# A fused attention and expert kernel: the listed order of every engine worked out anew, instructions unchanged

## The chip, the cores and the metric

One core of a Trainium2 chip runs the kernel. The metric is the device time of one execution in microseconds (us), and a result is the median of several executions. A profile of one more execution shows when each instruction ran on each engine: PE (TensorE), DVE (VectorE), ACT (ScalarE), POOL (GpSimd), and SP, which issues most transfers.

## What is computed

Three layers, one behind the other, for batch 4 and 576 positions. First windowed attention with 8 heads of width 64: heads 0 to 3 look at the last 32 positions, heads 4 to 7 at every fourth of the last 128. Then a channel mix with weights w_r (512 x 512), w_k (512 x 1024) and w_v (1024 x 512). Then causal attention in each of 4 experts, of which every position takes the best two by a gate.

```python
attn = softmax(where(mask, q @ k.T / 8, -1e9)) @ v          # per head
xk = mu_k * x + (1 - mu_k) * x_prev                          # x_prev: one position back
xr = mu_r * x + (1 - mu_r) * x_prev
y  = sigmoid(xr @ w_r) * (maximum(xk @ w_k, 0)**2 @ w_v)
out = sum over the top 2 experts e of  w_e * (softmax(causal(q_e @ k_e.T / 8)) @ v_e) @ wo_e
```

## The kernel before

**Tiling and stages.** The work goes batch by batch. In the first layer two heads share a tile (a head pair, numbered 0 to 3 within a batch; pairs 0 and 1 plain, 2 and 3 dilated). For each pair q and k are turned on PE (`qt`, `kt`, L398), the mask is written into the bank of the scores by a product (`sc<-masks`, L445), the scores are added (L452), ACT takes exponentials (L492), DVE normalises (`pe`, L504), PE turns the probabilities (`pt`, L532), ACT copies them out (`pts`, L533), PE multiplies with v (`av<-pts,vw`, L544), and ACT copies the result to the tile `x` (L559). For batch 0 nothing else can run beside it, and PE gets 52 fillers (`keep_warm`, L226, products `idle<-still` whose result nobody reads): 16 at the start and 36 in between.

In the second layer a product of float32 operands is made of three products in a shorter format: high by high, high by low, low by high (`product`, L689). x is mixed to `m` (ACT L663, DVE L664) and split into `xh` (ACT L666) and `xl` (DVE or POOL L667). Weights are split once, on arrival, in parts of 1024 columns: ACT prepares a part (L829), DVE shifts and joins it (L831, L832), ACT casts the high half (`wr_hi`, `wk_hi`, `wv_hi`, L837), DVE subtracts to get the low half (L838). The parts of w_r have the numbers 253 (first half of the columns) and 255 (second) in the listings below; 273 and 308 are the first two of the four parts of w_k. `z_c_f` is the product with w_r for half c of the positions and output tile f (the number behind it is the tile's own); a tanh on ACT (L712) makes the sigmoid of it. `h_c_f` is the product with w_k, f from 0 to 7, two tiles for each part of w_k; a relu on ACT (L718), the square on DVE or ACT, and a split to `kh` and `kl` follow (L720 to L728). `v` is the product with w_v (L734 evacuates it). `z` and `h` of batch 0 take banks of PSUM in turn, so that an `h` can start only when what stood in its bank has been read.

The third layer follows batch by batch, interleaved with the second layer of the batches behind: queries, keys and values (L689, L1038), scores (L1132, L1134), softmax (L1138, L1144), turns (L1196), sums (L1242), the output product (L1328), the results (`ob`, L1336) and their transfers.

**What sets the order.** The function writes the instructions in one program order, and the framework adds the waits by what they read and write. At its very end `issue_in_order` (L154) takes for each engine a list of numbers from the dictionary `ORDER` (L22), which names all its instructions by their place in the program, and binds each to issue right behind the one listed ahead of it. An engine issues strictly in that order: when the first instruction in its list has to wait, all behind it wait too. The list of SP does the same for the queue of transfers. How early something runs is thus a matter of two things only: its place in the list, and what it waits for.

```python
for engine, runs in ORDER.items():
    mine = [i for i in traced if str(i.engine) == "EngineType." + engine]
...
                if behind is not None:
                    tc.add_manual_dep(mine[n], behind.name, ..., reason="order of issue")
                behind = mine[n]
```

Of the kernel before, what the change touches and what calls it, by code (L numbers as in the profile page):

```python
# [27 lines left out]
    ),  # L28
    "DVE": (
# [29 lines left out]
    ),  # L59
# [1370 lines left out]
```

## Time and profile before

| | us |
|---|---|
| median of 3 runs | 528.67 |
| lowest, highest | 528.35, 530.55 |
| the profiled execution | 530.05 |
| its span, first to last instruction | 528.3 |

The mean granted clock of the profiled execution is 0.997 of full speed. The profiled execution's time is 1.75 us longer than its span, for what lies around it. Busy times in the page are sums over the span: matmuls overlap, and their ends are modelled, so a busy PE is not PE at its peak. In a timeline an idle time in brackets is that of the engine just before the instruction, with what ended it. A chain of waits is followed back from the last instruction to what released it at each step; here PE has 93% of it, DVE 4%, ACT 2%.

### The profile page before, as it was taken

How to read it: one execution, taken by the hardware profiler on the slowest of the kernel's cores; microseconds unless marked ns; L12 is line 12 of the kernel's file. 1: busy time of each engine (PE TensorE's matmuls, PEld its weight loads, DVE VectorE, ACT ScalarE, POOL GpSimd, SP SyncE). 2: the span in 40 equal slices, each digit the busy share in tenths (PEclk: the TensorE clock that was granted, in tenths of full speed). 3: DMA queues.
4: the chain of work that ended last, by engine and by line, in shares of the span. 5: the costliest groups of instructions: out<-in, count | busy, mean ns of one | idle time of the engine just before them, and what ended most of it. 6: DMA issues, size and time to landing. Idle time of an engine off the chain costs nothing.

```text
span 528.3 us, 12513 instructions
## 1 busy us (share of the span) xinstructions
PE 518.8 (98%) x4634; PEld 469.6 (89%) x4634; DVE 345.0 (65%) x1136; ACT 333.4 (63%) x945; POOL 97.8 (19%) x169
## 2 busy tenths in 40 slices
PE   8999899999999999999999999999999999999996
PEld 4679799999999999999999999999987798888873
DVE  3789999786793686474542517449686866766542
ACT  2799999677983585754634616238756865665661
POOL 8400000011441121410122313002303502313000
PEclk9999899999999999999999999999999999999999
DMA  9969386877635654320100420054614333452512
GB/s 168 239 206 298 100 215 138 151 138 146 138 92 132 144 113 113 81 68 34 37 0 1 101 62 1 1 136 110 161 36 101 117 100 73 109 130 49 167 61 99
DMA packets 130172, 57.64 MB, mean 109 GB/s; under 512 B 109928, under 2 KB 117184, under 8 KB 130112
## 3 DMA queue, kind: packets, MB, share of 16 engines
q1 hardware_dynamic: 129392, 55.88, 44.8%
q8 instruction: 36, 0.59, 0.5%
q0 software_dynamic: 416, 0.44, 0.4%
q10 hardware_dynamic: 304, 0.53, 0.3%
q14 instruction: 24, 0.20, 0.1%
HBM read 34.42 MB, written 10.03 MB: 84 GB/s over the span
## 4 chain that ended last, share of the span: by engine, by line
PE 93%; DVE 4%; ACT 2%; issue 1%; DVEq 0%; ACTq 0%
PE v L689 19%; PE h L689 18%; PE z L689 8%; PE av L1242 5%; PE pv L1038 5%; PE po L1328 5%; PE pq L689 5%; PE pk L689 5%; PE pt L1196 4%; PE av L544 4%; PE sc L1132 3%; PE sc L1134 3%; PE idle L226 3%; PE sc L468 2%; PE pt L532 2%; PE sc L452 1%
## 5 line engine op out<-in xcount | busy, mean ns | idle before, releaser
L689 PE MATMUL h<-xh,wk_hi 128*128 128x288 f32 x256 | 77.3, 303 | 1.2 <-ACT wk_hi L837 0.6
L689 PE MATMUL h<-xh,wk_lo 128*128 128x288 f32 x256 | 76.0, 297 | 1.0 <-DVE wk_lo L838 1.0
L689 PE MATMUL h<-xl,wk_hi 128*128 128x288 f32 x256 | 76.4, 299 | 0.3 <-DVE xl L667 0.3
L689 PE MATMUL v<-kh,wv_hi 128*128 128x288 f32 x256 | 76.1, 301 | 0.0
L689 PE MATMUL v<-kl,wv_hi 128*128 128x288 f32 x256 | 75.5, 297 | 0.1
L689 PE MATMUL v<-kh,wv_lo 128*128 128x288 f32 x256 | 74.3, 296 | 0.0
L679 POOL TENSOR_TENSOR xl<-m,xh 128x576 fp32r<-128x576 f32 x24 | 34.8, 1467 | 132.4 <-ACT xh L678 97.5
L1162 POOL TENSOR_SCALAR first<-pe,st 128x64 f32<-128x64 f32 x70 | 33.4, 527 | 132.4 <-DVE st L1156 89.9
L689 PEld LDWEIGHTS h<-xh,wk_hi 128*128 128x128 f32 x256 | 48.6, 190 | 2.7 <-ACT wk_hi L837 0.8
L1144 ACT ACTIVATE pe<-pe,st 128x320 f32<-128x320 f32 (+4 forms) x80 | 44.7, 560 | 8.4 <-DVE st L1138 8.1
L689 PEld LDWEIGHTS h<-xh,wk_lo 128*128 128x128 f32 x256 | 48.9, 191 | 1.2 <-DVE wk_lo L838 1.2
L689 PEld LDWEIGHTS h<-xl,wk_hi 128*128 128x128 f32 x256 | 48.8, 190 | 0.5 <-DVE xl L667 0.5
L689 PEld LDWEIGHTS v<-kl,wv_hi 128*128 128x128 f32 x256 | 48.0, 188 | 0.5 <-DVE kl L728 0.5
L689 PEld LDWEIGHTS v<-kh,wv_hi 128*128 128x128 f32 x256 | 48.0, 188 | 0.4
L689 PEld LDWEIGHTS v<-kh,wv_lo 128*128 128x128 f32 x256 | 47.8, 188 | 0.1
L664 DVE SCALAR_TENSOR_TENSOR m<-x,mus,m 128x288 f32<-128x288 f32 x64 | 30.3, 510 | 20.2 <-ACT m L663 20.2
L1138 DVE CUSTOM_DVE_ANT_0 pe<-sc,cmask 128x64 f32<-128x64 f32 (+4 forms) x80 | 33.1, 427 | 14.5 <-PE sc L1134 14.0
L718 ACT ACTIVATE r<-h 128x288 f32<-128x288 f32 x64 | 25.6, 408 | 26.6 <-PE h L689 22.1
L492 ACT ACTIVATE pe<-pe,st 128x96 f32<-128x96 f32 x108 | 39.1, 364 | 3.5 <-DVE st L487 3.3
L728 DVE TENSOR_TENSOR kl<-r,kh 128x288 fp32r<-128x288 f32 x50 | 28.5, 572 | 14.2 <-ACT kh L726 13.9
L689 PE MATMUL z<-xh,wr_hi 128*128 128x288 f32 x128 | 37.6, 298 | 0.0
L689 PE MATMUL z<-xl,wr_hi 128*128 128x288 f32 x128 | 37.5, 296 | 0.0
(201 smaller groups left out, 1423.6 us busy)
## 6 DMA issues: line engine op xcount, KB each, us to landing
kk<-kh SPq DMA_DIRECT2D x32, 144.0 KB, 2.7
kl<-kl SPq DMA_DIRECT2D x32, 144.0 KB, 2.7
raw_in_moe_w_k_dram<-in_moe_w_k_dram SPq DMA_DIRECT2D x4, 1024.0 KB, 10.2
raw_in_moe_w_v_dram<-in_moe_w_v_dram SPq DMA_DIRECT2D x4, 1024.0 KB, 6.4
out_dram<-ob SPq DMA_DIRECT2D x14, 256.0 KB, 2.0
rqk<-in_q_dram SPq DMA_DIRECT2D x48, 72.0 KB, 2.9
rqk<-in_k_dram SPq DMA_DIRECT2D x48, 72.0 KB, 2.5
moved<-turned SPq DMA_DIRECT2D x8, 432.0 KB, 2.9
```

What stands on the lines that cost most here:

```text
L492: nc.scalar.activation(pe[:, t, :], pe[:, t, :] if b else sc[:, c0 : c0 + WK], AF.Exp, bias=st[:, 0, t : t + 1], scale=-1.0, accum_out=st[ ...
L664: nc.vector.scalar_tensor_tensor(out=m, in0=x, scalar=mus[:, 0, w, f : f + 1], in1=m, op0=ALU.mult, op1=ALU.add)
L679: nc.gpsimd.tensor_sub(lo[:, f], m[:, f], hi[:, f].bitcast(F32))
L689: marks["product"] = nc.tensor.matmul(o, w[:, kt, wsl], x[:, kt, :], start=(n == 0), stop=(n == last)).ins
L718: nc.scalar.activation(r, p, AF.Relu)
L728: half.tensor_sub(kl[:, fo, :], r, kh[:, fo, :].bitcast(F32))
L1038: nc.tensor.matmul(p, x[:, kt, t0 : t0 + tn], w[:, kt, 512:772], start=(n == 0), stop=(n == 3 * KT - 1))
L1138: nc.vector.tensor_tensor_reduce(out=pe[:tn, PO[t] + c0 : PO[t] + c1], in0=sc, in1=m, scale=-0.125, scalar=(BIG if i == 0 else st[:tn, 1, ...
L1144: nc.scalar.activation(pb, pb, AF.Exp, bias=st[:tn, 0, t : t + 1], scale=-1.0, accum_out=st[:tn, 2, t : t + 1])
L1162: nc.gpsimd.tensor_scalar_mul(first["keys"][:, t, e % 2, :], pe[:, PO[t] : PO[t] + 64], st[:, 3, t : t + 1])
L1242: ins = nc.tensor.matmul(av1[p0 : p0 + 64, q0 - 64 : q1 - 64], vh[kb][:kn], w[:kn, c0 : c0 + q1 - q0], start=(kb == blocks[0]), stop=(kb = ...
L1328: nc.tensor.matmul(sums[t], x[:, t0 : t0 + 128], w[:, h, :], start=(h == 0 and n == 0), stop=(h == 1 and n == 2))
```

## The change

Only the dictionary `ORDER` differs: the lists of POOL, DVE, PE and ACT are other permutations of the same numbers. The list of SP, 355 entries, stands in another place in the dictionary and reads the same from first to last. Out of the longest common order fall 62 of 165 entries on POOL, 302 of 932 on DVE, 960 of 3924 on PE and 256 of 740 on ACT; an entry moves by at most 24, 41, 109 and 23 places. Instructions, tiles and buffers are the same. In the code of the change everything stands three lines lower (L692 is L689 of before). Of the diff two lines say all that can be read from it:

```diff
 ORDER = {
     "Pool": (
-        "0 2 1 40 7 19 33 20 12 26 37 10 8 11 9 3 16 4 38 42 39 5 41 6 34 21 35 23 36 22 27 43 24 28 25 44 29-30 17 "
+        "42 7 0 40 1 26 33 2 19 3 5 4 6 41 10 8 12 11 9 13 34 16 35 17 36 20 18 21 30 37 23 38 24 39 27 25 14 22 15 "
...
```

Three places, and two smaller ones. On ACT, at the end of batch 0's attention, where w_r is split, the order before is:

```order
L559 COPY x_212<-av_2_288_644 128x2x144
L829 ACTIVATE raw_in_moe_w_r_dram_253<-raw_in_moe_w_r_dram_253 128x1024
L533 COPY pts_3_0_762<-pt_3_0_761 96x384
L829 ACTIVATE raw_in_moe_w_r_dram_255<-raw_in_moe_w_r_dram_255 128x1024
L533 COPY pts_3_1_784<-pt_3_1_783 96x384
L837 CAST wr_hi<-raw_in_moe_w_r_dram_253 128x4x256
L559 COPY x_212<-av_3_0_767 128x2x144
L533 COPY pts_3_2_804<-pt_3_2_803 96x384
L837 CAST wr_hi<-raw_in_moe_w_r_dram_255 128x4x256
L559 COPY x_212<-av_3_288_794 128x2x144
```

and in the change:

```order
L536 COPY pts_3_0_762<-pt_3_0_761 96x384
L562 COPY x_212<-av_2_288_644 128x2x144
L536 COPY pts_3_1_784<-pt_3_1_783 96x384
L832 ACTIVATE raw_in_moe_w_r_dram_255<-raw_in_moe_w_r_dram_255 128x1024
L562 COPY x_212<-av_3_0_767 128x2x144
L832 ACTIVATE raw_in_moe_w_r_dram_253<-raw_in_moe_w_r_dram_253 128x1024
L840 CAST wr_hi<-raw_in_moe_w_r_dram_255 128x4x256
L536 COPY pts_3_2_804<-pt_3_2_803 96x384
L840 CAST wr_hi<-raw_in_moe_w_r_dram_253 128x4x256
L562 COPY x_212<-av_3_288_794 128x2x144
```

Before, the preparation of part 253 stands ahead of the copy pts_3_0 and that of 255 ahead of pts_3_1; now both stand behind pts_3_1, and part 255 is prepared and cast ahead of 253.

On PE, at the same time, where the attention of batch 0 ends and the first product z begins, the order before is:

```order
L544 MATMUL av_3_0_767<-pts_3_1_784,vw_3_257 64x32 x2
L226 LDWEIGHTS still
L226 MATMUL idle<-still 128x512
...
L689 MATMUL z_0_0_860<-xh_0_0_280,wr_hi 128x288
L689 MATMUL z_0_0_860<-xl_0_0_281,wr_hi 128x288
L689 MATMUL z_0_1_874<-xh_0_0_280,wr_hi 128x288
L689 MATMUL z_0_1_874<-xl_0_0_281,wr_hi 128x288
L544 MATMUL av_3_288_794<-pts_3_1_784,vw_3_257 64x32 x2
```

and in the change:

```order
L547 MATMUL av_3_0_767<-pts_3_0_762,vw_3_257 64x64 x6
L547 MATMUL av_3_0_767<-pts_3_1_784,vw_3_257 64x64 x2
L547 MATMUL av_3_0_767<-pts_3_1_784,vw_3_257 64x32 x2
L547 MATMUL av_3_288_794<-pts_3_1_784,vw_3_257 64x32 x2
L547 MATMUL av_3_288_794<-pts_3_1_784,vw_3_257 64x64 x2
L547 MATMUL av_3_288_794<-pts_3_2_804,vw_3_257 64x64 x6
L692 MATMUL z_0_0_860<-xh_0_0_280,wr_hi 128x288
L692 MATMUL z_0_0_860<-xl_0_0_281,wr_hi 128x288
```

Before, fillers stand among the last products of the attention, and four products z go ahead of the last av; now all of the attention is done first, and the fillers, as many as before, stand earlier.

On PE, where z ends and h begins, the order before is:

```order
L689 MATMUL h_0_0_1029<-xh_0_2_924,wk_hi 128x288
L689 MATMUL h_0_0_1029<-xl_0_2_925,wk_hi 128x288
L689 MATMUL h_0_0_1029<-xh_0_2_924,wk_lo 128x288
L689 MATMUL h_0_2_1072<-xh_0_2_924,wk_hi 128x288
L689 MATMUL h_0_2_1072<-xl_0_2_925,wk_hi 128x288
L689 MATMUL h_0_2_1072<-xh_0_2_924,wk_lo 128x288
```

and in the change:

```order
L692 MATMUL z_1_2_976<-xh_1_1_282,wr_hi 128x288
L692 MATMUL z_1_2_976<-xl_1_1_283,wr_hi 128x288
L692 MATMUL z_1_2_976<-xh_1_1_282,wr_lo 128x288
L692 MATMUL h_0_0_1029<-xh_0_2_924,wk_hi 128x288
L692 MATMUL h_0_0_1029<-xl_0_2_925,wk_hi 128x288
L692 MATMUL h_0_0_1029<-xh_0_2_924,wk_lo 128x288
L692 MATMUL h_0_1_1054<-xh_0_2_924,wk_hi 128x288
L692 MATMUL h_0_1_1054<-xl_0_2_925,wk_hi 128x288
L692 MATMUL h_0_1_1054<-xh_0_2_924,wk_lo 128x288
```

Before, h_0_0 is followed by h_0_2, which needs the second part of w_k (308). Now three products of z_1_2 have moved between those of h_0_0, and h_0_1 follows, which needs only the first part (273), then three products of h_0_2.

The two smaller places: in the first two head pairs of batch 0 the mask products stand ahead of the transposes of k (and, for the first pair, of q), and the first `pt` ahead of the scores of the second pair. On POOL all masks come first, and 13 transfers of v that stood among them come behind.

## Rows read from the trace of the kernel before

**Rows 1.** The page: busy time of each engine, share of the span, instructions.

```profile
PE 518.8 (98%) x4634; PEld 469.6 (89%) x4634; DVE 345.0 (65%) x1136; ACT 333.4 (63%) x945; POOL 97.8 (19%) x169
```

**Rows 2.** Stretches: start and end, length, busy time by engine, then PE clock, DMA share, GB/s.

```profile
40.00:50.00 10.00, 10.00 (x94) 9.05 (x94) 9.10 (x17) 9.72 (x20) 0.00 (x0) 1.00 1.03 321
50.00:60.00 10.00, 8.36 (x57) 7.45 (x56) 10.00 (x16) 9.90 (x21) 0.00 (x0) 1.00 0.37 83
60.00:70.00 10.00, 9.31 (x55) 9.02 (x56) 9.18 (x15) 8.85 (x19) 0.00 (x0) 0.83 0.60 196
520.00:529.00 9.00, 3.72 (x25) 2.12 (x21) 2.31 (x5) 1.83 (x5) 0.00 (x0) 0.96 0.44 147
```

**Rows 3.** PE's waits: who waits, for whom, us in total, times, longest.

```profile
PE idle L226 <- DVE still L219: 1.2, 1, 1.2
PE h L689 <- DVE wk_lo L838: 1.0, 1, 1.0
...
PE kt L398 <- DVE masks L298: 0.4, 1, 0.4
...
PE h L689 <- ACT r L718: 0.2, 1, 0.2
```

**Rows 4.** Stretches of two microseconds, columns as in rows 2.

```profile
56.00:58.00 2.00, 1.70 (x11) 1.49 (x12) 2.00 (x4) 1.91 (x4) 0.00 (x0) 1.00 0.00 0
58.00:60.00 2.00, 0.87 (x5) 0.41 (x3) 2.00 (x3) 2.00 (x5) 0.00 (x0) 1.00 0.00 0
62.00:64.00 2.00, 2.00 (x10) 2.00 (x9) 2.00 (x3) 2.00 (x4) 0.00 (x0) 0.50 1.01 351
```

**Rows 5.** PE's timeline: start, us, engine, line, operation, count, idle time before it.

```profile
41.57 0.48 PE L689 MATMUL z<-xh,wr_hi 128*128 128x288 f32 x1
...
55.92 0.40 PE L689 MATMUL h<-xh,wk_hi 128*128 128x288 f32 x1 [0.21 <-ACT xh L666]
...
58.94 0.40 PE L689 MATMUL h<-xh,wk_hi 128*128 128x288 f32 x1 [0.59 <-ACT wk_hi L837]
...
60.45 0.41 PE L689 MATMUL h<-xh,wk_lo 128*128 128x288 f32 x1 [0.98 <-DVE wk_lo L838]
...
64.88 0.29 PE L689 MATMUL h<-xh,wk_lo 128*128 128x288 f32 x1
```

**Rows 6.** The chain that ended last: start, us, what.

```profile
205.58 12.78 PE z L689 x96
```

**Rows 7.** PE's timeline, batch 0, scores of the second head pair and first pt.

```profile
15.65 1.04 PE L452 MATMUL sc<-kT,qT 64*64 64x96 f32 x20
16.63 0.53 PE L532 MATMUL pt<-ident,pe 128*96 128x128 f32 x3
```

**Rows 8.** Timeline of GpSimd and PE: last transfer of v issued, first use.

```profile
19.40 0.64 POOL L370 DMA_DIRECT2D vw<-in_v_dram  x1 [0.32 <-DMA vw<-in_v_dram]
...
32.66 0.34 PE L544 MATMUL av<-pts,vw 96*64 96x64 f32 x4
```

**Rows 9.** ACT's timeline around the splitting of w_r.

```profile
37.19 1.16 ACT L829 ACTIVATE raw_in_moe_w_r_dram<-raw_in_moe_w_r_dram 128x1024 f32<-128x1024 f32 x1
...
39.77 0.47 ACT L533 COPY pts<-pt 96x384 f32<-96x384 f32 x1
40.15 1.19 ACT L837 CAST wr_hi<-raw_in_moe_w_r_dram 128x1024 fp32r<-128x1024 f32 x1
41.21 0.71 ACT L559 COPY x<-av 128x288 f32<-128x288 f32 x1
41.70 0.54 ACT L533 COPY pts<-pt 96x384 f32<-96x384 f32 x1
...
43.71 1.37 ACT L663 ACTIVATE m<-x,mus 128x288 f32<-128x288 f32 x3
45.03 1.29 ACT L666 CAST xh<-m 128x288 fp32r<-128x288 f32 x3
```

**Rows 10.** ACT's timeline, the first relu of h that it waits for.

```profile
66.81 0.41 ACT L718 ACTIVATE r<-h 128x288 f32<-128x288 f32 x1 [1.11 <-PE h L689]
```

More of the change, by code (lines that the diff above doesn't have):

```diff
@@ L22 @@
     "Pool": (
[5 rows of a table removed]
[5 rows of a table added]
     ),
     "DVE": (
[29 rows of a table removed]
[30 rows of a table added]
     ),
     "PE": (
[55 rows of a table removed]
-    ),
-    "Activation": (
[25 rows of a table removed]
[57 rows of a table added]
     ),
@@ L149 @@
         "280-293 296 294-295 297-320 323 321-322 324-354"
+    ),
+    "Activation": (
[25 rows of a table added]
     ),
```

229 rows, old and new, of the table ORDER are left out of this document.

## Prediction

> **What bounds the kernel now.** I read the share of busy time first: TensorE (PE) is busy 98% of the span of 528.3 us, VectorE (DVE) and ScalarE (ACT) two thirds [rows 1]. A new order can win only time in which PE idles or runs slowly, so its idle time is the budget: 528.3 - 518.8 = 9.5 us. Of this 5.3 us lie in the last nine microseconds (9.00 less 3.72 busy, [rows 2]) and 1.2 us before the first filler [rows 3]; the last instructions and the first keep their places. That leaves 3.0 us, and the slices of 50 to 70 us alone idle 1.64 + 0.69 = 2.3 us [rows 2]. The list of PE's waits agrees: after that first wait the longest are for wk_lo and wk_hi, 0.98 and 0.59, both in this stretch [rows 3, 5]. It is also the one stretch with a low granted clock, 0.83 as a mean of ten microseconds [rows 2], and 0.50, which is the 1.2 GHz level, in 62 to 64 us [rows 4]. From 60.45 to 64.88 us 22 products start, 21 steps in 4.43 us [rows 5]; at the full level products follow each other by 12.78/96 = 0.133 us [rows 6], so 21 steps would take 2.8 us, and the fall of the clock costs 1.6. So the most that any order can win by removing idle time and half clock in the middle is 3.0 + 1.6 = 4.6 us, 0.9%. Everything else that the change moves must lie under PE's work, or it costs.
>
> **The change part by part.**
>
> *Start, 7 to 17 us.* On PE the mask products of the first two head pairs go ahead of the transposes, and the first transposed probabilities (pt) ahead of the second pair's scores. The 0.4 us wait for masks [rows 3] can go, less the transposes that covered the rest: I take -0.2. The second move has a price: before, the scores start at 15.65 and the pt at 16.63 [rows 7], so PE, held to its order, would stand for up to 1.0 us until the same pt can go. DVE and ACT set the pace of batch 0, and 36 fillers stand in PE's list for its idle time. Walking DVE's rows in the new order up to the third pair's scores leaves +0.1. Bounds 0 and +1.0; I take +0.1.
>
> *GpSimd's list.* Thirteen of its transfers of v now follow all masks. They were issued up to 19.40 us, and PE first multiplies with tiles from them near 32.66 us [rows 8]; masks are only brought forward. At nothing; if the 13 us of cover were gone, each microsecond would be paid. SP's list is unchanged, so no transfer leaves that queue earlier.
>
> *Splitting w_r, 37 to 46 us.* This is the dearest move. Before, ACT prepared the first half at 37.19, ahead of copies (pts, x), and made wr_hi at 40.15 to 41.34; the first product z followed at 41.57 [rows 5, 9]. Now both preparations stand behind the last-but-one pts, the second half is first, and the half that z begins with comes last. From that pts at 39.77 ACT has pts, preparation, copy x, preparation, cast, pts, cast: 0.47 + 1.16 + 0.71 + 1.16 + 1.19 + 0.54 + 1.19 = 6.4 us [rows 9]; each starts about 0.1 before the one ahead ends, so 5.7, and the last cast ends at 45.5. With the 0.23 us of before from cast to product, z starts at 45.7, 4.1 us later. Fillers that stood here now stand earlier, so PE is all but idle from about 41 to 45.7.
>
> *What the delay is worth.* Before, z was over just before 55.92, and the first 36 products h took from there to 65.0 for 36 x 0.133 = 4.8 us of work [rows 5]. Now z, 96 products, ends at 45.7 + 12.8 = 58.5. By then ACT, which starts the mix m at 46.1 instead of 43.71, has made up one m (1.37/3) and one xh (1.29/3) that the new order does in idle time before [rows 9]: it is late by 2.4 - 0.9, say 1.4 us. The second part of wk_hi, released at 58.94, comes at 60.3, and wk_lo, released at 60.45, at 61.8 [rows 5]. The new PE order no longer needs these next: it puts nine products of h_0_1, which use the first part, behind h_0_0. That bank waits for a tanh at about 60.7; PE reaches it at 58.5 + 1.6 = 60.1, waits 0.6, and ends the same 36 products at 63.9, against 65.0: **-1.1 us at full clock**.
>
> *The clock.* In 56 to 60 us PE was busy 1.70 and 0.87 of two microseconds each, no single wait was over 1.0 us, and the clock was at its lower level right after [rows 4, 5]. From 41 to 45.7 PE has some 1.3 us of work (pt and av). By that row the clock falls here too, and z begins at the lower level: +1.6 us if it lasts as long. The 0.6 us wait is then covered, and the 36 products end at 58.5 + 1.6 + 4.8 = 64.9: **-0.1 us**. I take this value; the ends are -1.1 and, if a second fall follows at 60 us as before, -0.1 + 1.6 = +1.5. The Trainium skill (TensorE: Matmul & The Clock Gate, "HAM oscillation — how this bites in real kernels") describes one cause, a long unbroken wait between groups of matmuls, after which the next group starts at the lower clock; it speaks against this change, which makes such a wait, and by it alone z starts slow and the clock holds at 60 us: -0.1. The rows of 56 to 60 us, several short waits, show that a long unbroken wait is not needed; by them a fall at 60 us is possible too, +1.5.
>
> *ACT's lag.* 1.4 us late, it meets its next wait at 66.81, where it had idled 1.11 us for PE [rows 10]. So 0.3 us stays, and PE waited for ACT right there, 0.2 us for r [rows 3]. Taken: +0.3. Bounds: 0, and the whole 2.4 us of ACT if nothing is absorbed.
>
> *The rest.* From 70 us to the end the lists are permuted by some places everywhere, with the same instructions, and PE has there 3.0 - 2.3 = 0.7 us of idle to win, less what the first 50 us hold. New short waits are as likely. Taken: 0, bounds -0.7 and +1.6 (one half-clock stretch).
>
> **Sum.** -0.2 + 0.1 + 0 - 0.1 + 0.3 + 0 = +0.1 us against the profiled execution's 530.05 us, which is 1.4 us above the median of the three runs, 528.67. I put the sum on the median, and add 0.2 us for the walk's own optimism (it has no wait that the rows do not show): 528.67 + 0.1 + 0.2, **529.0 us**.
>
> **The rivals.** A measurement of this kernel tells about 0.5%, 2.6 us, from no change.
>
> *Slower: ACT becomes the bound from 41 to 85 us.* For it: ACT is busy 9.72, 9.90 and 8.85 of each ten microseconds from 40 to 70 [rows 2], so it has little room to catch up. Against it: the 1.11 us above. If its 2.4 us of delay reach PE and both falls of clock come: 2.4 + 1.5 = +3.9, 532.6 us. It decides once ACT is more than 1.1 us late at the first relu that PE waits for, which is all of its idle time there. Other new waits in the 450 us behind, each with a half-clock stretch of 1.6, lead to 534. Chance 0.26.
>
> *Faster: the walk underrates the new order.* No fall of the clock at 45 us, -1.1 there, the 0.4 us for masks, the 0.7 us of later idle time and ACT's 0.3 and 0.2 not paid: -2.2, and up to the limit of 4.6, so 524.1 to 526.5, likeliest 525.5. For it: h_0_1 fills just the waits that are there now. Against: it needs all of the budget, in a stretch where the order begins by losing 4.1 us. Chance 0.22.
>
> *The change does not do what it says.* The transfer list is the same, so no landing moves except v's on GpSimd's queue, which nobody waits for: 528.7, inside "same". This case has 0.12, the sum above 0.40: 0.52 together.
>
> **How the numbers follow.** Predicted 529.0. The range goes down to 525.3, where the faster case has its bulk, and up to 533.0, beyond the 532.6 of the slower one; about one in ten is left out on each side. Within "same" alone it would be 527 to 531. Faster 0.22, same 0.52, slower 0.26.
>
> **What would show it.** z's first product near 45.7 instead of 41.57, with PE idle before it. A granted clock under 1.00 in 44 to 50 us and 1.00 in 60 to 70. No wait for wk_hi or wk_lo. The first relu of h_0_1 within half a microsecond of 66.8. The chain of waits still PE by 93%. Wrong if z starts before 43, if PE's waits in 70 to 520 us sum to over 3 us, or if ACT waits for nothing in 60 to 70 us.

## The result, and the profile after

The changed kernel takes 535.65 us (median of 4, 534.27 to 535.82) against 529.61 (median of 4, 528.35 to 531.26): a ratio of 1.0106, 95% interval 1.0069 to 1.0144. It is **slower by 1.1%**, some 5 to 6 us, where 529.0, no change, was forecast. The old kernel's median over these four executions is 0.9 us higher than over the three that the forecast started from. The changed kernel's profiled execution, 534.27 us, is the shortest of its four, and its span is 4.3 us longer than that of before.

The busy times [rows 1] have hardly moved, as they must with the same instructions:

```profile
PE 517.2 (97%) x4630; PEld 468.9 (88%) x4634; DVE 343.1 (64%) x1136; ACT 334.2 (63%) x945; POOL 95.6 (18%) x169
```

The stretches of the changed kernel, columns as in [rows 2, 4]: the place with little work on PE and a low clock (0.50 is the 1.2 GHz level) has moved from 56 to 64 us to 40 to 49 us.

```profile
40.00:50.00 10.00, 6.39 (x63) 6.00 (x64) 7.53 (x10) 8.52 (x14) 0.00 (x0) 0.83 1.00 314
46.00:48.00 2.00, 2.00 (x11) 2.00 (x10) 1.93 (x5) 1.54 (x4) 0.00 (x0) 0.50 1.18 271
60.00:70.00 10.00, 9.31 (x67) 8.61 (x66) 10.00 (x16) 9.68 (x20) 0.00 (x0) 1.00 0.34 107
80.00:90.00 10.00, 9.16 (x75) 8.47 (x78) 9.10 (x15) 9.22 (x22) 0.10 (x1) 1.00 0.80 181
```

PE is busy 6.39 of ten microseconds at 40 to 50 us, where it had no idle time before, and 60 to 70 us is at the full clock now. A new loss is at 80 to 90 us: 9.16, against 9.89 before.

PE's waits for wk_lo and wk_hi are gone, as forecast. Nine waits that sum to over 0.4 us are new against [rows 3]. Six of them are in PE's timeline (to compare with [rows 5]), the other three in the list below it:

```profile
41.95 0.45 PE L547 MATMUL av<-pts,vw 96*64 96x32 f32 x8 [1.14 <-ACT x L562]
44.31 0.57 PE L547 MATMUL av<-pts,vw 96*64 96x64 f32 x12 [1.91 <-ACT pts L536]
45.41 0.61 PE L692 MATMUL z<-xh,wr_hi 128*128 128x288 f32 x1 [0.53 <-ACT wr_hi L840]
...
48.70 0.32 PE L692 MATMUL z<-xh,wr_lo 128*128 128x288 f32 x1
...
62.12 0.40 PE L692 MATMUL h<-xh,wk_hi 128*128 128x288 f32 x1 [0.51 <-ACT z L715]
...
84.78 0.40 PE L692 MATMUL h<-xh,wk_hi 128*128 128x288 f32 x1 [0.84 <-ACT r L721]
...
101.65 0.56 PE L547 MATMUL av<-pts,vw 96*64 96x64 f32 x12 [0.63 <-DMA vw<-in_v_dram]
```

```profile
PE sc L1137 <- DMA kl<-kl: 0.7, 1, 0.7
PE av L547 <- DMA rqk<-moved: 0.7, 2, 0.3
PE sc L448 <- ACT pe L495: 0.6, 1, 0.6
```

The first two of the list lie behind 130 us, the wait of `sc` for `pe` at 13.43 us, in the front. The first three of the timeline are PE's stand before z. z begins at 45.41 instead of 41.57. From 45.41 to 48.70 there are 13 steps in 3.29 us, 0.25 each, instead of 13 x 0.133 = 1.7: the fall of the clock. h_0_1 waits 0.51 us for its tanh at 62.12. At 84.78 PE waits for a relu of ACT and at 101.65 for a transfer of v. The wait for the relu belongs to the new lists and not to the lateness: every kernel below that has the new lists from 62 to 85 us waits there for 0.82 to 0.88 us, also those in which PE is 3 us ahead.

ACT's timeline at the end of the split (to compare with [rows 9]), then one line of before:

```profile
44.19 1.17 ACT L840 CAST wr_hi<-raw_in_moe_w_r_dram 128x1024 fp32r<-128x1024 f32 x1
...
45.71 0.96 ACT L666 ACTIVATE m<-x,mus 128x288 f32<-128x288 f32 x2
...
50.37 0.41 ACT L715 ACTIVATE z<-z 128x288 f32<-128x288 f32 x1 [1.36 <-PE z L692]
...
51.34 1.19 ACT L832 ACTIVATE raw_in_moe_w_k_dram<-raw_in_moe_w_k_dram 128x1024 f32<-128x1024 f32 x1
```

```profile
48.46 1.18 ACT L829 ACTIVATE raw_in_moe_w_k_dram<-raw_in_moe_w_k_dram 128x1024 f32<-128x1024 f32 x1
```

The last cast of wr_hi ends at 45.36. The mix m starts at 45.71 instead of 43.71. Then ACT, bound to its list, stands 1.36 us for the first tanh, because z is both late and slow, and the preparation of w_k's first part begins at 51.34, where before it began at 48.46: **ACT is 2.9 us late**.

**The chain.** The chain that ended last goes by PE for 93% of the span before, and for 78% in the change. That share alone says little: in e12 below it is 76%, and e12 is as fast as before. What tells is where the chain runs behind the first tanh. Before:

```profile
47.50 0.41 ACT z L712
...
59.26 1.15 DVE wk_lo L838
...
60.45 6.33 PE h L689 x34
```

and in the change:

```profile
45.41 4.94 PE z L692 x24
50.37 0.41 ACT z L715
...
66.60 2.28 DVE wk_lo L841 x2
...
68.93 15.03 PE h L692 x110
```

In both kernels it leaves PE at this tanh and comes back to it at a product h behind wk_lo. In between lie, before, 11.5 of 13 us on DVE, which prepares w_k there, and in the change 12.8 us on DVE and over 4 on ACT, of 18.6. So by the chain it was not PE that set the pace from 48 to 60 us before either. The change starts this stretch 2.87 us later.

**How late PE is.** A single wait tells little of the end, since a late engine may catch up. So I added up, instruction by instruction, the usual spacing of PE's work without the fillers (medians by kind of instruction over the compared traces), and looked how much later each kernel had done as much as the old one had at a given time. The same can be done for ACT by its durations. Microseconds, one profiled execution each; a minus is ahead of before. Single executions differ by about a microsecond in the first 30 us already, and that much of a column is chance: of e12's lead of 3.6 us at 67 us, 1.1 stand at 30 us, where its lists are still the old ones. The profiled execution of e3 is the longest of its ten, 2.0 us above their median:

| time of before, us | change | e2 | e4 | e3 | e12 | e9 |
|---|---|---|---|---|---|---|
| PE at 30 | -0.3 | -0.4 | 0.4 | 0.4 | -1.1 | -0.2 |
| PE at 45 | 4.2 | 4.2 | 3.3 | 0.5 | -1.1 | -0.2 |
| PE at 60 | 3.2 | 4.2 | 2.5 | 0.5 | -0.8 | 0.1 |
| PE at 67 | 0.4 | 4.1 | -0.3 | 0.4 | -3.6 | -2.7 |
| PE at 80 | 0.5 | 4.1 | -0.2 | 0.5 | -3.5 | -0.7 |
| PE at 100 | 2.7 | 4.3 | 2.2 | 0.6 | -1.7 | -0.2 |
| PE at 130 | 2.6 | 4.3 | 2.2 | 1.1 | -1.2 | -0.2 |
| PE at 220 | 4.1 | 4.5 | 2.6 | 2.7 | 0.0 | -0.3 |
| ACT at 60 | 2.9 | 4.2 | 2.3 | 0.5 | -1.1 | -0.1 |
| ACT at 68 | 1.8 | 4.1 | 1.1 | 0.5 | -2.2 | -1.2 |
| ACT at 130 | 2.7 | 4.3 | 2.2 | 1.1 | -1.2 | -0.2 |

The column of the change holds the whole case. PE loses 4.2 us before z, wins all but 0.4 back by 67 us, as the prediction said, and then loses it a second time, without a great wait anywhere: 2.6 us late at 130 us, where ACT is 2.7 late too, and 4.1 at 220 us. The other columns are those of the experiments.

### The profile page after: what moved, and what is told of

Read it like the earlier page. It is cut to its first block, busy times and chain, and to the rows that moved or that the text cites. A ratio compares the mean times of both kernels' runs of the same rounds, so it can differ in the third digit from the quotient of the medians.

```text
span 532.6 us, 12517 instructions
## 1 busy us (share of the span) xinstructions
PE 517.2 (97%) x4630; PEld 468.9 (88%) x4634; DVE 343.1 (64%) x1136; ACT 334.2 (63%) x945; POOL 95.6 (18%) x169
## 4 chain that ended last, share of the span: by engine, by line
PE 78%; DVE 8%; ACT 4%; DMA 4%; issue 2%; SPq 2%; POOL 1%; DVEq 0%; ACTq 0%; POOLq 0%
PE v L692 15%; PE h L692 13%; PE z L692 8%; PE pv L1041 5%; PE po L1331 4%; PE pk L692 4%; PE pq L692 4%; PE pt L1199 4%; PE av L1245 4%; PE av L547 4%; PE idle L229 2%; PE sc L1137 2%; PE sc L1135 2%; PE sc L471 2%; SPq L1023 2%
## 5 line engine op out<-in xcount | busy, mean ns | idle before, releaser
L692 PE MATMUL h<-xh,wk_hi 128*128 128x288 f32 x256 | 76.2, 300 | 1.4 <-ACT r L721 0.8
L692 PE MATMUL v<-kh,wv_hi 128*128 128x288 f32 x256 | 76.3, 302 | 0.1
L692 PE MATMUL h<-xl,wk_hi 128*128 128x288 f32 x256 | 75.8, 296 | 0.0
L692 PE MATMUL h<-xh,wk_lo 128*128 128x288 f32 x256 | 75.3, 295 | 0.1
L692 PE MATMUL v<-kl,wv_hi 128*128 128x288 f32 x256 | 75.4, 297 | 0.0
L692 PE MATMUL v<-kh,wv_lo 128*128 128x288 f32 x256 | 74.3, 295 | 0.0
L1165 POOL TENSOR_SCALAR first<-pe,st 128x64 f32<-128x64 f32 x70 | 31.2, 485 | 137.2 <-DVE st L1159 70.4
L1147 ACT ACTIVATE pe<-pe,st 128x192 f32<-128x192 f32 (+4 forms) x80 | 45.0, 563 | 10.9 <-DVE st L1141 9.1
L692 PEld LDWEIGHTS h<-xh,wk_hi 128*128 128x128 f32 x256 | 47.8, 187 | 2.7 <-ACT r L721 1.1
L692 PEld LDWEIGHTS v<-kh,wv_hi 128*128 128x128 f32 x256 | 47.9, 188 | 1.2 <-DVE r L728 0.3
L692 PEld LDWEIGHTS h<-xh,wk_lo 128*128 128x128 f32 x256 | 48.2, 188 | 0.4 <-DVE wk_lo L841 0.4
L692 PEld LDWEIGHTS v<-kl,wv_hi 128*128 128x128 f32 x256 | 48.1, 188 | 0.3 <-DVE kl L731 0.2
L692 PEld LDWEIGHTS h<-xl,wk_hi 128*128 128x128 f32 x256 | 48.1, 188 | 0.2
L692 PEld LDWEIGHTS v<-kh,wv_lo 128*128 128x128 f32 x256 | 47.8, 188 | 0.1
L1141 DVE CUSTOM_DVE_ANT_0 pe<-sc,cmask 128x192 f32<-128x192 f32 (+4 forms) x80 | 33.1, 427 | 13.9 <-PE sc L1137 11.9
L692 PE MATMUL z<-xh,wr_hi 128*128 128x288 f32 x128 | 38.4, 304 | 0.5 <-ACT wr_hi L840 0.5
L692 PE MATMUL z<-xl,wr_hi 128*128 128x288 f32 x128 | 38.5, 302 | 0.0
L692 PE MATMUL z<-xh,wr_lo 128*128 128x288 f32 x128 | 37.6, 298 | 0.0
```

The source lines that it names most:

```text
L692: marks["product"] = nc.tensor.matmul(o, w[:, kt, wsl], x[:, kt, :], start=(n == 0), stop=(n == last)).ins
L1141: nc.vector.tensor_tensor_reduce(out=pe[:tn, PO[t] + c0 : PO[t] + c1], in0=sc, in1=m, scale=-0.125, scalar=(BIG if i == 0 else st[:tn, 1, ...
L1147: nc.scalar.activation(pb, pb, AF.Exp, bias=st[:tn, 0, t : t + 1], scale=-1.0, accum_out=st[:tn, 2, t : t + 1])
L1165: nc.gpsimd.tensor_scalar_mul(first["keys"][:, t, e % 2, :], pe[:, PO[t] : PO[t] + 64], st[:, 3, t : t + 1])
```

## The experiments

**Theory A**: the loss is made before z, by the late split of w_r and the fall of the clock. **Theory B**: it is made by the many small moves behind. **Theory C**, which came up with the first results: from 40 to 90 us ACT and DVE set the pace, so that what PE wins there does not count and what they lose does.

Most kernels take the old lists up to some time, and the new ones behind, or the reverse. Each engine's list is cut where that trace stood at that time, and the second list gives the rest in its own order:

```python
def cut(first, n, second):       # n: how many entries of each engine's first list
    return {e: first[e][:n[e]] + [x for x in second[e] if x not in set(first[e][:n[e]])] for e in first}
```

### e1 and e2: old up to z and new behind, and the reverse

```diff
+ORDER = cut(OLD, {"Pool": 56, "DVE": 74, "PE": 293, "Activation": 65, "SP": 36}, NEW)   # e1
+ORDER = cut(NEW, {"Pool": 56, "DVE": 78, "PE": 305, "Activation": 70, "SP": 37}, OLD)   # e2
```

> Every engine follows the old lists up to 41.5 us of the old trace (first product z) and the new ones from there on. Theory A (the loss is made before z: w_r split late, z 3.8 us late, clock down for 3.4 us): the loss is mostly gone, +0 to +2 us against before; no wait of PE over 1 us in 40 to 50 us. Theory B (the loss is made by the many small moves behind z): it stays, +4 to +6 us.

> The counterpart: the new lists up to the first product z (45.4 us of the changed kernel's trace), the old ones from there on. Theory A: slower than the change itself or like it, +5 to +7 us against before, since the old order behind z also loses its 4 us at 56 to 64 us. Theory B: about +1 to +2 us.

Measured: e1 532.44 us, ratio 1.0058 (1.004 to 1.0076); e2 536.03 us, 1.0124 (1.0092 to 1.0155), before 528.97 us. e2 is as theory A has it: the new front alone makes a loss as large as the change's; that it is larger is within the intervals. It has both falls of the clock:

```profile
40.00:50.00 10.00, 6.40 (x63) 5.74 (x64) 7.51 (x10) 8.36 (x14) 0.00 (x0) 0.83 0.97 299
60.00:70.00 10.00, 8.06 (x43) 7.38 (x44) 10.00 (x14) 9.72 (x18) 0.00 (x0) 0.83 0.33 106
```

Its column in the table stays at 4.1 to 4.5 from 45 us to the end: with the old lists behind z nothing is won back and nothing lost. e1 lies between the theories. Its cut is not clean: in the new lists all of the attention goes ahead of z, so at 41.5 us part of it is left over, and PE still waits 2.4 us there.

```profile
PE av L549 <- ACT pts L538: 2.4, 2, 2.2
```

### e3, e6, e12: old up to 80, 200 and 58.5 us, new behind

```diff
+ORDER = cut(OLD, {"Pool": 56, "DVE": 133, "PE": 545, "Activation": 134, "SP": 59}, NEW)    # e3
+ORDER = cut(OLD, {"Pool": 77, "DVE": 376, "PE": 1602, "Activation": 343, "SP": 191}, NEW)  # e6
+ORDER = cut(OLD, {"Pool": 56, "DVE": 101, "PE": 413, "Activation": 97, "SP": 45}, NEW)     # e12
```

> The old lists up to 80 us of the old trace, the new ones behind. Theory A: within 1 us of before. Theory B, as the trace counts it (waits of PE at 84, 101, 110 to 130, 165 to 210 and 420 to 460 us, some 3 us more than before): +2.5 to +4 us.

> The old lists up to 200 us, the new ones behind. If the 2 us that the new order loses behind 80 us are lost between 80 and 180 us, as the lag of PE behind before says: -0.5 to +0.5 us. If they are spread to the end: +1 us.

> The old lists up to 58.5 us and the new ones from there on, a seam without an instruction on the wrong side. It is the change without its front. If the front's delay of ACT is the whole loss before 130 us: -1 to +1 us against before. If the new order behind 58.5 us has waits of its own at 84 and 101 us, whatever comes before: +1 to +2.5 us.

Measured: e3 530.28 us, 1.002 (1.0002 to 1.0038); e6 530.34 us, 1.0006 (0.999 to 1.0021); e12 530.04 us, 1.0006 (0.9991 to 1.0022). At 58.5 us of the old trace and 61.5 us of the new one, old and new lists have issued exactly the same instructions on every engine. e12 is therefore the change without its front and nothing else, and its time is that of before within 1.2 us: **the loss is made ahead of that point, all but a microsecond of it.** Behind it both kernels run the same lists, and the change is behind e12 by 4.0 us on PE and on ACT at 60 us, 4.0 at 67, 3.8 at 130, 4.1 at 220 us: a delay of all engines at the seam is passed on to the end in full. (0.8 of the 4.0 us stand at 30 us already.) Theory B keeps a small part. From 130 to 220 us the change, e3 and e12, which have the new lists there, lose 1.2 to 1.6 us of PE's time and e4 0.4, while e2 and e9, which have the old ones, lose 0.2 at most. In the time e3 puts 1 us on it: without their gain at 58 to 67 us, the new lists behind 80 us lose 0.2%.

e12 shows a second thing. Its stretches:

```profile
60.00:70.00 10.00, 9.86 (x73) 9.39 (x72) 10.00 (x18) 9.13 (x18) 0.00 (x0) 1.00 0.73 244
...
80.00:90.00 10.00, 9.09 (x89) 8.12 (x90) 8.74 (x22) 8.41 (x24) 0.10 (x1) 1.00 0.65 147
```

The half clock of 60 to 70 us is gone, and PE wins 2.5 us between 30 and 67 us (-1.1 to -3.6). At 130 us it is at -1.2 again, and at 220 us there is nothing left. The lead was real, and worth nothing. The listed waits of PE in 80 to 105 us, 0.83 us for the relu and 0.34 for ACT's m, make up about half of what it gives back there; the rest is in no listed wait. The chain has left PE in this stretch:

```profile
70.47 1.24 DVE wv_lo L843
...
78.05 7.79 DMA rqk<-in_q_dram
...
89.64 3.06 PE v L694 x21
```

DVE's low half of w_v is followed by six microseconds in the queue of transfers and by the landing of q, then by DVE again, which turns to qT, pe and x, and only then by PE.

### e10: old up to 33.5 us, new behind

```diff
+ORDER = cut(OLD, {"Pool": 56, "DVE": 62, "PE": 236, "Activation": 50, "SP": 30}, NEW)
```

> The old lists up to 33.5 us, where old and new differ in fillers alone, the new ones behind. In the changed kernel's profile the new front cost nothing at 30 us (PE's lag -0.25), but PE is busy 8.6 of 10 us at 10 to 20 us, and one profile with that front shows a granted clock of 0.83 there and PE 2.2 us late. If that happens in many executions: 1 to 2 us below the changed kernel. If it is rare: the changed kernel's time within 0.7 us.

Measured: 534.71 us, ratio 1.0089 (1.0067 to 1.0112), within the interval of the change, 1.0069 to 1.0144. The moves of masks, transposes and pt in the first 33 us account for little, as far as these intervals can tell. With e12 the place of the loss is 33.5 to 58.5 us.

### e4, e11, e15: fillers into PE's stand, the first tanh later, both

```diff
-            keep_warm(3 if n > 17 else 1)
+            keep_warm(19 if n == 23 else 3 if n > 17 else 1)
```

On PE, 5 of the 16 new fillers go behind av_3_0, 9 behind the first four instructions of av_3_288, 2 ahead of z (e4). On ACT one entry goes three places back (e11); e15 has both.

```diff
     "Activation":
-... 53 74 54 75 55 76 87 56 77 78 92 94 90 ...
+... 53 74 54 75 55 76 56 77 78 87 92 94 90 ...
```

> The changed kernel with 16 more fillers on PE, where it stands from 40.6 to 45.4 us: 5, 9 and 2. It prices the fall of the clock alone. If the late z and the clock matter for the end: the clock stays at its upper level at 45 to 49 us, z begins at the same 45.4 to 45.7 us, its first 13 steps take 0.133 instead of 0.24, and the time is 1.0 to 1.6 us below the changed kernel. If ACT's lag sets the end instead: no change, the 1.4 us turn into waits of PE for ACT's r and z before 90 us.

> The changed kernel with one entry moved: on ACT the first tanh of z goes three places back, behind two casts xh and the preparation of w_k's first part. In the change ACT stands there 1.36 us for z. If this wait makes ACT's lag (2.9 us at 50 us instead of the 1.4 of the prediction) and the lag makes the waits behind 80 us: ACT's lag at 52 us is 1.5 to 1.9 us, and the time 0.8 to 1.4 us below the changed kernel. If PE's own lag makes them: no change.

> The changed kernel with the 16 fillers at 41 to 45 us and the first tanh three places later on ACT. If the fall of the clock and ACT's wait for z are two parts of the delay at the seam: below each alone, +1 to +2 us against before. If the tanh costs only because z starts at the lower clock: like the fillers alone, +2.5 to +3.5 us. What is then left is the late end of w_r's split itself, 1.4 to 1.6 us of ACT at 46 us.

Measured: e4 531.78 us, ratio 1.0057 (1.0033 to 1.0081); e11 533.58 us, 1.0076 (1.0057 to 1.0095); e15 532.59 us, 1.0062 (1.0041 to 1.0084). The fillers take about half of the loss away, 1.0106 - 1.0057 = 0.5%, 2.6 us; the two intervals together leave some 0.2 to 5 us, so it can't be told from the 1.6 that PE loses by the clock. z still begins late, at 46.02 us in e4, but at the full clock (compare 46 to 48 us above):

```profile
40.00:50.00 10.00, 9.80 (x89) 6.89 (x88) 7.35 (x10) 9.44 (x18) 0.00 (x0) 1.00 0.98 306
46.00:48.00 2.00, 2.00 (x16) 1.98 (x16) 2.00 (x3) 1.59 (x4) 0.00 (x0) 1.00 1.10 251
```

ACT's first tanh then comes at 49.67 without a listed wait, 0.7 us earlier than in the change although this execution is 0.7 us behind it at 30 us: the 1.36 us were a consequence of the fall, and moving the tanh on top of the fillers wins nothing (e15 is like e4). Without the fillers that move does not win anything clear either: e11 is 0.3% below the change, within the noise. What is left with the fillers is the late split: in e4 ACT is 2.2 us late at 46 us and stays so to 62 us, and 0.57% is lost.

### e8: the split of w_r where it was

```diff
     "Activation":
-... 47 48 49 67 50 70 68 71 51 69 72 52 73 ...
+... 47 48 49 50 51 67 68 70 52 71 72 69 73 ...
     "DVE":
-... 72 78 79 80 59 81 60 ...
+... 72 78 59 79 80 60 81 ...
```

> The changed kernel with one thing undone: on ACT and DVE the two parts of w_r are prepared, cast and subtracted where they were (13 entries on ACT and 7 on DVE change places among themselves). Theory A: z begins at 41.5 to 43 us, the clock holds, and the time is 2.5 to 4 us below the changed kernel, +2 to +3 us against before; if ACT then sets the pace, PE's lag at 80 us is negative and the wait for r at 84 us is longer than 0.84 us.

Measured: 534.81 us, ratio 1.0098 (1.006 to 1.0136): no difference from the change that can be measured. The expectation fails. z begins at 45.84, no earlier, because now the copies of the attention are late, and in the new list of PE all of the attention goes ahead of z. PE's waits:

```profile
PE pt L537 <- ACT pts L538: 1.6, 1, 1.6
...
PE av L549 <- ACT x L564: 1.0, 1, 1.0
```

So the place of the split on ACT is not the cause alone. That it is so together with PE's new order, attention first and then z, with no fillers between, is what these waits suggest; the kernel that would show it, the new split with PE's old order, was not run.

### e7: fillers, and the old lists behind 80.5 us

```diff
+ORDER = with_16_fillers(cut(NEW, {"Pool": 56, "DVE": 132, "PE": 546, "Activation": 133, "SP": 58}, OLD))
```

> The changed kernel with the 16 fillers at 41 to 45 us, and the old lists for all that it does behind 80.5 us. If the loss is the fall of the clock (2.6 us) and what the new order loses behind 80 us (2 to 3 us), both are gone: -0.5 to +1 us against before. If the late z itself costs: +2 to +3 us.

Measured: 535.56 us, ratio 1.0112 (1.0084 to 1.0139). Neither end that was expected. Its profile, the longest of the four executions by 2.1 us, has the clock low twice: at 16 to 20 us (last section), behind which all engines are 2 us late, and at 80 to 90 us.

```profile
80.00:90.00 10.00, 6.89 (x36) 6.56 (x35) 8.21 (x14) 7.59 (x16) 0.10 (x1) 0.73 0.82 179
```

PE waits 3.1 us there for a relu that ACT does at 84.92 us, behind the second of two casts of w_v in the old list, and that cast waits 1.29 us for DVE. So it does not tell what the fillers alone are worth with the old lists.

### e5, e9, e13, e14: only the gain at 58 to 67 us

Could one keep the lead of e12? Old lists, then the new ones up to 80.5 (e5), 72 (e9), 85.5 (e13) and 133 us (e14) of the changed kernel's trace, then the old ones:

```diff
+MID = cut(OLD, {"Pool": 56, "DVE": 101, "PE": 413, "Activation": 97, "SP": 45}, NEW)      # e5: 55.5 us; DVE 97, PE 401, Activation 93
+ORDER = cut(MID, {"Pool": 56, "DVE": 132, "PE": 546, "Activation": 133, "SP": 58}, OLD)   # e5
+ORDER = cut(MID, {"Pool": 56, "DVE": 119, "PE": 482, "Activation": 118, "SP": 48}, OLD)   # e9
+ORDER = cut(MID, {"Pool": 56, "DVE": 137, "PE": 574, "Activation": 143, "SP": 64}, OLD)   # e13
+ORDER = cut(MID, {"Pool": 61, "DVE": 251, "PE": 1005, "Activation": 229, "SP": 126}, OLD) # e14
```

> The old lists up to 55.5 us, the new ones for what the changed kernel does up to 80.5 us (h_0_1 right behind h_0_0 among them), the old ones from there on. Theory A (the new order of 55 to 80 us is a gain that the rest hides): PE 2 to 3.5 us ahead of before at 67 us, no clock under 1.00 in 60 to 70 us, and -1 to -3 us in the time. Theory C (ACT sets the pace of 40 to 90 us): PE is ahead at 67 us, waits for ACT's r between 80 and 90 us, and the time is that of before within 1 us.

> The old lists up to 58.5 us, where old and new have issued exactly the same instructions, the new ones up to 72 us of the changed kernel's trace (h_0_1 behind h_0_0), the old ones from there on. It takes from the change only what fills PE's waits at 58 to 61 us. If ACT's pace decides (theory C): PE is 3 us ahead at 67 us, ACT 1.5 to 2 us ahead at 70 us, since it no longer idles for PE at 66.8, and only ACT's lead is left behind 90 us: -1 to -2 us against before, faster than both kernels. If the lead of PE counts: -3 us. If a wait for r follows and the clock falls as with the old lists from 80.5 us on: +2 us.

> The old lists up to 58.5 us, the new ones up to 85.5 us of the changed kernel's trace, the old ones from there on. Behind 58.5 us the new lists bring PE 2.8 us ahead at 67 us, and still 1.1 us at 85, and the new lists behind give it back. If the old lists behind 85 us keep it: -1 us against before, ACT and PE both ahead by 1 us at 130 us. If ACT or DVE hold PE to the old pace there too: no difference.

> The same with the second seam at 133 us, where old and new lists have issued the same instructions but one: PE, ACT and DVE were 0.1 us ahead there, counted from the first seam, to 1.2 us ahead, counted from before. Kept: 0 to -1 us against before. It tells how much of the 3.5 us that the new lists give back is lost behind 133 us.

Measured: e5 532.46 us, ratio 1.0044 (1.0025 to 1.0062); e9 529.61, 1.0006 (0.9994 to 1.0019); e13 530.80, 1.0031 (1.0018 to 1.0043); e14 530.52, 1.0018 (1.0003 to 1.0033). None beats the old kernel. In each PE is 2.5 to 3.3 us ahead at 67 us. e5 shows most plainly where it goes. PE's wait, ACT behind it, and the stretch:

```profile
80.54 0.61 PE L693 MATMUL h<-xh,wk_hi 128*128 128x288 f32 x1 [3.08 <-ACT r L722]
```

```profile
79.07 1.11 ACT L841 CAST wv_hi<-raw_in_moe_w_v_dram 128x1024 fp32r<-128x1024 f32 x1 [1.29 <-DVE raw_in_moe_w_v_dram L836]
80.08 0.41 ACT L722 ACTIVATE r<-h 128x288 f32<-128x288 f32 x1
```

```profile
80.00:90.00 10.00, 9.46 (x78) 9.06 (x79) 6.95 (x29) 6.61 (x23) 0.11 (x1) 0.67 0.55 135
```

The relu for which PE waits 3.08 us comes at 80.08 us on ACT. In the old kernel the relu behind the casts of w_v began at 79.81 us, in ACT's timeline:

```profile
77.56 2.35 ACT L837 CAST wv_hi<-raw_in_moe_w_v_dram 128x1024 fp32r<-128x1024 f32 x2
79.81 0.71 ACT L718 ACTIVATE r<-h 128x288 f32<-128x288 f32 x2
```

ACT is where it always was, and PE's lead only makes it wait longer. The wait is followed by a fall of the clock, 0.67 at 80 to 90 us, and at 85 us the lead of 3.2 has become a lag of 2.6 us. e9 meets the same wait earlier, ACT itself held by DVE:

```profile
72.01 0.40 PE L691 MATMUL h<-xh,wk_hi 128*128 128x288 f32 x1 [1.60 <-ACT r L720]
```

```profile
70.24 1.11 ACT L839 CAST wv_hi<-raw_in_moe_w_v_dram 128x1024 fp32r<-128x1024 f32 x1 [1.02 <-DVE raw_in_moe_w_v_dram L834]
```

Behind it the chain of e9 runs over DVE and ACT until PE goes on, and it goes on when the old kernel does, 0.2 us earlier, as much as e9 was ahead at 30 us. Before, then e9:

```profile
80.27 3.85 PE h L689 x27
```

```profile
80.07 3.85 PE h L691 x27
```

In e13 PE's lead is spent in waits for ACT and, at 83.53, for DVE:

```profile
81.16 0.40 PE L693 MATMUL h<-xh,wk_hi 128*128 128x288 f32 x1 [0.83 <-ACT r L722]
...
83.53 1.88 PE L472 MATMUL sc<-kT,qT 64*64 64x96 f32 x36 [1.45 <-DVE kT L430]
```

e14 has the first of these waits, 0.84 us at 81.91, and behind it two for transfers of v, 0.59 us at 98.71 and, behind the second seam, 1.23 us at 137.34.

All this bears theory C out, with DVE and the transfers beside ACT: where PE is ahead between 67 and 130 us, it gives the lead back, and the waits and the chains of e9 and e12 lead to ACT, to DVE and to the transfers behind DVE's work. In e9 ACT too was ahead, by 1.2 us at 68 us, and lost it to DVE by 80 us. A faster kernel would have to take work from DVE and ACT here. That was not tried, and it would be the direct test of the theory.

## Why the prediction was wrong

- **Start, 7 to 17 us: taken -0.1 together, not contradicted.** PE was 0.3 us ahead at 30 us, where single executions differ by more than that. GpSimd's list at nothing: right, no wait for its masks; the wait of 0.63 us for v at 101 us is SP's queue, not GpSimd's.
- **The split of w_r: right in size.** z was forecast at 45.7 and began at 45.41.
- **The clock: right for PE.** A fall of 1.6 us, 3.29 against 1.7 measured, and none at 60 us. The row of 56 to 60 us carried it. The Trainium skill (TensorE: Matmul & The Clock Gate, "HAM oscillation — how this bites in real kernels") agrees in what came of it: behind the stand z ran at the lower level, 0.50 at 46 to 48 us, and after the wait of 0.51 us at 62.12 the clock held. The stand was not one unbroken wait, though, but three, of 1.14, 1.91 and 0.53 us, with products between.
- **What the delay is worth: the step that failed.** The term was -0.1: the late z, 4.1 us, was to be made good on PE by what h_0_1 fills, and the 36 products to end 0.1 us ahead of before. On PE that nearly came, 0.4 us behind at 67 us. The prediction took this for the state of the kernel. It was that of one engine, and of one that did not set the pace there: the same gain is worth nothing in e12 and e9, and the delay at the seam arrives at the end in full, 4.1 us.
- **ACT's lag: the same step on the other side.** It was put at 1.4 us, of which 0.3 was to stay. The trace has 2.9 us. Nearly all of the missing 1.5 is the wait for the first tanh, 1.36 us: the fall of the clock had been priced for PE alone, and ACT, in its listed order, stands behind the slow z with all that PE will need later. The 1.11 us of idle time [rows 10] did take up as much at first, 1.8 us at 68, but at 130 us ACT is 2.7 late again. DVE, busy for all of 50 to 60 us [rows 2], had no term at all, and the chain runs over it.
- **The rest behind 70 us: taken 0, bounds -0.7 to +1.6, measured +3.7 on PE** (0.5 at 80 us, 4.1 at 220). e12 loses as much, 3.5 us, with the same lists in the same stretch, and is no slower than before: for the most part it is the lead won at 58 to 67 us that is spent there, and 1.2 us (e12) and 1.5 us (the change) are lost behind 130 us. With the old lists behind (e2), which neither win nor lose, the delay at the seam arrives just the same.
- **Its signs.** z came near 45.7, the clock and the waits for wk_hi and wk_lo were as said. The chain did not stay PE's by 93%. And one of the signs of being wrong came: in 60 to 70 us ACT waits for nothing but 0.18 us for DVE.
- **The rivals.** The slower one named the mechanism, ACT as the bound from 41 to 85 us, though not DVE. The wait by which it would reach PE, at the first relu, is not how it came: the wait for a relu at 84.78 is in e12 too. Its chance, 0.26, was too low: ACT was busy 9.7 to 9.9 of ten microseconds from 40 to 60 us and DVE 9.1 to 10.0 [rows 2], and one idle microsecond at 66.8 us is no reason to let 1.4 of delay go. Its price, 532.6, was too low too; the range ended at 533.0.

The faster rival was wrong for the same cause: it counted PE's idle time at 56 to 64 us as the budget. e12 and e9 removed that idle time and the half clock, and the time did not move.

What stays open: three of the changed kernel's four executions are 1.4 us longer than the profiled one, so the profile shows 4.3 of the 5 to 6 us. A second fall of the clock in the front, as e7's profile has one, could be the reason in some; the mean clocks of the three, 0.992 to 0.994, against 0.994 of the profiled one, do not settle it. Which of the moves between 33.5 and 58.5 us makes how much of the delay, beside the fall of the clock, was not separated either.

## What to carry to other kernels

Before an engine's idle time is counted as a gain, look which engines are full in that stretch, and where the chain runs in it: an engine at 98% over the whole span can be the one that waits in 50 us of it, and a lead there is spent at the next hand-over. A delay is priced on all engines at one seam, a point where both orders have issued the same instructions, and what the fullest of them is late there arrives, in this case, at the end. A fall of the clock is to be priced on every engine that waits, in its fixed list, for the slow work: here 1.36 us on ACT beside the 1.6 on PE.

## What was not expected of the hardware

With the same lists, the clock fell in the front of one execution and not in that of another. The changed kernel, then e7, which has the same lists there:

```profile
8.00:16.00 8.00, 6.43 (x66) 4.16 (x66) 5.75 (x14) 4.53 (x15) 5.90 (x19) 1.00 1.36 184
16.00:20.00 4.00, 3.84 (x63) 3.22 (x62) 3.47 (x14) 2.59 (x13) 3.31 (x6) 1.00 1.32 177
```

```profile
8.00:16.00 8.00, 6.51 (x70) 4.35 (x70) 5.48 (x14) 4.14 (x15) 6.33 (x20) 1.00 1.36 194
16.00:20.00 4.00, 3.92 (x41) 3.20 (x40) 2.27 (x9) 0.84 (x3) 2.91 (x5) 0.57 1.31 189
```

Up to 16 us PE was busy for 6.43 and 6.51 of 8 us, at the full clock in both, and the waits over 0.15 us in 8 to 16.5 us were the same four, 0.31, 0.16, 0.64 and 0.36 us in the change and within 0.01 of that in e7, which was 0.8 us later by then. Then the clock of e7 fell to a mean of 0.57 and that of the change did not. No row here shows why. The busy time behind the fall is no help in comparing them, since products at the lower level last longer.

And nine kernels with the same lists up to 33.5 us had PE between 1.1 us ahead and 0.6 us behind the old trace at 30 us: single profiles of this kernel differ by over a microsecond before anything has been changed.
